# Six places for the down weights, gate products on GpSimd, and a wait ahead of each pair's inverse data, in an adaLN block of state-space convolution and gated feed-forward

## The chip, the cores and the metric

The kernel runs on one core of a Trainium2 chip. The metric is the device time of one execution in microseconds. The engines are named as the profile names them: PE is TensorE (PEld its weight load), DVE is VectorE, ACT is ScalarE, POOL is GpSimd, and SP is SyncE, whose queue issues nearly all transfers.

## The reference

The inputs are 2,048 tokens of 640 channels in float32. Cut to what matters:

```python
sa, ca, ga, sb, cb, gb = (silu(c) @ w_mod) split in six rows of 640
h = layernorm(x) * (1 + ca) + sa
x = x + ga * (causal_conv(h, K) + h * D_skip)     # K from the state-space parameters, conv by rfft/irfft of 4096
h = layernorm(x) * (1 + cb) + sb
gate, up = h @ w1, h @ w3                         # 640 -> 1728
x = x + gb * ((silu(gate) * up) @ w2)             # 1728 -> 640
```

All is float32. The kernel keeps that precision in the feed-forward part by splitting each operand in a high and a low part, so that each product is three matmuls: high by high, high by low, low by high.

## The kernel before, in words

**The convolution** takes the first 355 us. It is done channel block by channel block with transforms written as matmuls, and its instructions have an order written out by hand. The change touches nothing there. At its end the spectra's last transform step is still open: for each of 16 token slots (128 tokens each) the data lies in DRAM, in `zd`, and needs a last small product, which is added to the residual `x2`. Four consecutive slots make one block of 512 tokens. `inverse_load` (line 578 and after, transfers at line 589) fetches such data for some slots into the tile `low`, and `inverse` (line 593 and after) makes the products `iy` (line 604) and has DVE add them to `x2` (line 609). Slots 0 to 3, block 0, are done at once. Slots 4 to 15 are done as pairs of slots u = 2 to 7, inside the feed-forward of blocks 0 and 1.

**The feed-forward** treats blocks 0 and 1 in `ffn`. For each of 14 tiles of the 1,728 hidden columns (13 of 128, one of 64) it loads three weights (`wr` holds w1 and w3, `w2r` holds w2), splits them (ACT makes the high part `wh`, `w2h`; DVE the low part `wl`, `w2l`), makes gate and up in PSUM (`gu`, lines 1044 to 1046), gates them on ACT and DVE, and adds the tile's down product to five accumulators `acc` (line 1081). After each tile the function `between` is called. There, in block 0, tiles 2 to 7 and 9 to 13 each do half a pair by `inverse_half`, and block 1's first tile does the last half: an even call loads the pair's data (eight transfers) and makes the products of the first 320 channels, the odd one those of the other 320. Two pairs fit into `low` at once, as each pair uses the place `u % 2`. `between` also loads the residual `x` of blocks 2 and 3.

These loads go through `held_back`: they carry a wait for one matmul, `self.hold`, which is set once, to the last product of slots 0 to 3. `load_x2` (line 575) has it too.

**Blocks 2 and 3** are treated together. `pair_up` makes gate and up of both blocks with a scheme that saves products (lines 834 to 917), for which POOL makes sums of weights (lines 853 to 856). `pair_down` then makes the down products, first block 2's 14 tiles, then block 3's. Its weights w2 are loaded again: `load` fetches two at once into a tile `wq` of the tag `wr`, which has two such tiles, so that four weights have a place. The first four are asked for ahead of the loop; then, after each second weight is split, the next two. `weights2` splits a weight: ACT makes `w2h` (line 1029), DVE `w2l` (line 1033), each with two buffers. In block 3 the weight's first 512 columns are multiplied by the gate row `gb` before (line 1028, DVE), so that its output needs no gating.

**Block 2's output** is made by `output2`, called in the first round of block 3: ACT scales the last 128 columns, PE turns them, DVE multiplies four accumulators by the gate (line 1014) and adds the turned columns to the residual (line 1020). The four additions of line 1019 and the store (line 1018) are handed back as a list, one step to a round of block 3. Block 3's accumulators are two banks of the tag `gu` and the banks `acc0`, `acc1` and `acc4`.

**What sets the order.** Behind the convolution no order is written out. The framework puts each engine's instructions in a sequence by their priority (the program order) and by when it reckons them ready, so a load can be issued earlier than a call that stands ahead of it. Each engine, and SP's queue, then runs its sequence strictly in order.

Of the kernel before, what the change touches and what calls it, by code (L numbers as in the profile page):

```python
# [10 lines left out]
F32 = mybir.dt.float32  # L11
# [3 lines left out]
ALU = mybir.AluOpType  # L15
# [3 lines left out]
P = 128  # L19
L = 2048  # L20
D = 640
KT = D // P
# [150 lines left out]
class Plan:  # L173
# [4 lines left out]
    def add(self, name, eng, took, f, after=(), rank=0.0, port=False, take=(), give=(), table=None, dma=None):  # L178
        assert name not in self.tasks, name
        if not isinstance(eng, tuple):  # L180
            eng, f = (eng,), f and (lambda e, f=f: f())
        self.tasks[name] = (eng, f, tuple(after))
        self.takes[name] = [name + "'" * i for i, x in enumerate(take) if x[0] == "bank"]
        for tag, key in give:
            if tag == "bank":
                self.gives.setdefault(key, []).append(name)
# [24 lines left out]
class K:  # L211
# [402 lines left out]
    def inverse_half(self, i, ps, tag, bufs):  # L614

        u, h = 2 + i // 2, i % 2
        if h == 0:
            self.zu = self.inverse_load(u % 2 * 2560, 2 * u, 2, 0, D)
        self.inverse(2 * u, 2, self.zu, ps, tag, bufs, 0, D, h)


    def split(self, H, Lo, v, eng):
# [322 lines left out]
    def pair_down(self, wp, pool, ps, po):  # L945

        order = (0, 1, 2, 3, 13) + tuple(range(4, 13))
        pend = n = None
        late = []
        raw = {}  # L950
        todo = [(b, m) for b in (2, 3) for m in order]

        def load(i):
            if i % 2 == 0:
                t = self.wrp.tile([P, 2, KT, P], F32, name=f"wq{i}", tag="wr", bufs=2).rearrange("p a k f -> p a (k f)")
                for x in range(2):
                    b, m = todo[i + x]
                    raw[b, m] = t[:, x]
                    if m < 13:
                        self.nc.sync.dma_start(t[:, x], self.w2[m * P:(m + 1) * P, :])  # L960
                    else:
                        for y in range(2):
                            self.nc.sync.dma_start(t[y * 64:(y + 1) * 64, x], self.w2[1664:1728, :])
        load(0)
        load(2)
        for b in (2, 3):
            acc = None
            for m in order:
                w2h, w2l = self.weights2(b, m, wp, raw.pop((b, m)))
                i = todo.index((b, m)) + 3  # L970
                if i < len(todo):
                    load(i)
                if acc is None:
                    new = [po.tile([P, 512], F32, name=f"acc{b}{k}", tag=f"acc{k}") for k in range(KT)] if b == 2 else None
                if m < 13:
                    n = 0 if n is None else n + 1
                    t = self.slots[n % 4]
                    ah, al = t[:, :512], t[:, 512:]
                    self.split(ah, al, self.a.pop((m, b)), self.nc.vector)
                else:  # L980
                    ah, al = self.a.pop((m, b)), None
                end = (b, m) == (3, 12)
                if pend is not None:
                    self.down(*pend, *([(4, 0, 1, 2)] if end else []))
                    if acc is None and b == 3:
                        late = self.output2(pend[1], pool, ps)
                    elif late:
                        late.pop(0)()
                if acc is None:
                    acc = new or [ps.tile([P, 512], F32, name=f"acc3{k}", tag="gu", bufs=3) if k < 2 else  # L990
                                  po.tile([P, 512], F32, name=f"acc3{k}", tag=f"acc{(0, 0, 0, 1, 4)[k]}") for k in range(KT)]
                prev = pend
                pend = (m, acc, ah, al, w2h, w2l)
        real = self.nc
        nc = self.nc = Engines(self, real)
        self.down(*pend, (4, 0, 1))
        pt = self.turn_last(3, acc, ps)
        self.down(*pend, (2,))
        self.down(*prev, (3,))
        self.down(*pend, (3,))  # L1000
        self.output(3, acc, ps, pt)
        self.nc = real


    def output2(self, acc, pool, ps):

        nc = self.nc
        V = nc.vector
        x = self.x2[2]
        pt = self.turn_last(2, acc, ps)  # L1010
        y = [(pool.tile([P, 512], F32, name=f"y2{j}", tag="s", bufs=3) if j else
              self.keep.tile([P, 512], F32, name="og20", tag="og", bufs=2)) for j in range(4)]
        for j in range(4):
            V.tensor_mul(y[j], acc[j], self.gb)

        def store():
            for q in range(4):
                nc.sync.dma_start(self.ov[q, :, 8:12, :], x[q * 32:(q + 1) * 32])
        add = lambda j: V.tensor_add(x[:, j, :512], y[j], x[:, j, :512])
        V.tensor_add(x[:, :, 512:], pt, x[:, :, 512:])  # L1020
        return [lambda: add(0), lambda: add(1), lambda: add(2), lambda: add(3), store]

    def weights2(self, b, m, wp, w2r):

        nc = self.nc
        w2h, w2l = (wp.tile([P, D], F32R, name=f"w2{x}{b}_{m}", tag=f"w2{x}", bufs=2) for x in "hl")
        if b == 3:
            nc.vector.tensor_mul(w2r[:, :512], w2r[:, :512], self.gb)
        nc.scalar.activation(w2h, w2r, AF.Copy)
        q = slice(0, P if m < 13 else 64)  # L1030
        if m == 13:
            nc.gpsimd.memset(w2l[64:].bitcast(F32), 0.0)
        nc.vector.tensor_tensor(w2l[q], w2r[q], w2h[q].bitcast(F32), op=ALU.subtract)
        return w2h, w2l
# [914 lines left out]
```

## Time and profile before

| what | us |
|---|---|
| three timed runs | 944.38, 941.34, 939.71 |
| their median | 941.34 |
| the profiled execution | 938.05 |
| its span, from the first to the last instruction | 936.3 |

The profiled execution is one run of its own. Its span leaves out the 1.75 us that lie around the instructions. Times within the trace count from the span's start. By this clock the convolution ends near 355 us, `ffn` runs to near 660, `pair_up` to near 830, and `pair_down` to the end. The mean granted TensorE clock was 0.984. In rows of instructions the columns are start, duration, engine, line, operation, output from inputs, shape and count; a bracket holds the engine's idle time just before and what ended it.

### The profile page before, as it was taken

How to read it: one execution, taken by the hardware profiler on the slowest of the kernel's cores; microseconds unless marked ns; L12 is line 12 of the kernel's file. 1: busy time of each engine (PE TensorE's matmuls, PEld its weight loads, DVE VectorE, ACT ScalarE, POOL GpSimd, SP SyncE). 2: the span in 40 equal slices, each digit the busy share in tenths (PEclk: the TensorE clock that was granted, in tenths of full speed). 3: DMA queues.
4: the chain of work that ended last, by engine and by line, in shares of the span. 5: the costliest groups of instructions: out<-in, count | busy, mean ns of one | idle time of the engine just before them, and what ended most of it. 6: DMA issues, size and time to landing. Idle time of an engine off the chain costs nothing.

```text
span 936.3 us, 21994 instructions
## 1 busy us (share of the span) xinstructions
PE 846.5 (90%) x8983; PEld 673.8 (72%) x8983; DVE 693.9 (74%) x1228; ACT 518.7 (55%) x892; POOL 325.2 (35%) x323
## 2 busy tenths in 40 slices
PE   1266888999989988999999999999999999999997
PEld 1045767778778745677877788888888888888775
DVE  7899999999979756556765757465667777765753
ACT  5889999999887533423423335354333434444331
POOL 2398989998988261000000000001133333100000
PEclk9987999999999999999999999999999999999999
DMA  8966566232251469955533353231322122123342
GB/s 196 303 218 156 177 154 162 69 107 70 69 150 46 139 193 234 232 166 141 155 101 97 104 164 85 84 104 51 75 67 57 56 57 57 43 61 108 97 129 83
DMA packets 125005, 112.78 MB, mean 120 GB/s; under 512 B 12393, under 2 KB 107113, under 8 KB 123625
## 3 DMA queue, kind: packets, MB, share of 16 engines
q1 hardware_dynamic: 124136, 110.46, 42.6%
q8 instruction: 70, 1.15, 0.5%
q10 hardware_dynamic: 768, 0.92, 0.4%
q14 instruction: 31, 0.25, 0.1%
HBM read 90.38 MB, written 20.97 MB: 119 GB/s over the span
## 4 chain that ended last, share of the span: by engine, by line
PE 64%; DVE 8%; ACT 8%; DMA 7%; issue 3%; SPq 0%; POOL 0%; DVEq 0%; ACTq 0%
PE p L834 17%; PE acc L1081 16%; PE gu L1044 6%; PE gu L1046 6%; PE gu L1045 6%; PE ps L147 4%; ACT tr L147 2%; PE fz L147 2%; DMA low<-zd 2%; DVE fp L147 2%; DVE yy L147 2%; PE kps L147 2%; DMA wq<-in_w 2%; PE fk L147 1%; DMA x<-in_x 1%
## 5 line engine op out<-in xcount | busy, mean ns | idle before, releaser
L1044 PE MATMUL gu<-xh,wh 128*128 128x512 f32 x270 | 106.2, 398 | 2.8 <-ACT xh L623 1.4
L1046 PE MATMUL gu<-xh,wl 128*128 128x512 f32 x270 | 105.4, 391 | 0.0
L1045 PE MATMUL gu<-xl,wh 128*128 128x512 f32 x270 | 105.2, 390 | 0.0
L147 ACT ACTIVATE tr<-ph 128x512 f32<-128x512 f32 (+1 forms) x160 | 93.8, 603 | 8.8 <-POOL ph L147 3.9
L853 POOL TENSOR_TENSOR ws<-wp 128x256 f32<-128x256 f32 x13 | 9.6, 738 | 230.9 <-DMA wp<-in_w 116.0
L147 POOL TENSOR_TENSOR ph<-p,p 128x1024 int32<-128x1024 int32 x40 | 79.1, 1978 | 3.7 <-ACT tr L147 3.0
L147 DVE TENSOR_TENSOR yy<-yy,tr 128x512 f32<-128x512 f32 (+1 forms) x80 | 75.5, 946 | 2.6 <-ACT tr L147 2.3
L737 ACT ACTIVATE wh<-wr 128x640 fp32r<-128x640 f32 x51 | 34.9, 731 | 71.0 <-PE gu L1045 55.6
L834 PE MATMUL p<-x,wch 128*128 128x512 f32 x208 | 68.3, 389 | 0.0
L1044 PEld LDWEIGHTS gu<-xh,wh 128*128 128x128 f32 x270 | 50.6, 188 | 19.1 <-issue 2.1
L147 POOL TENSOR_TENSOR yy<-e,e 128x512 f32<-128x512 f32 x48 | 52.6, 1107 | 23.6 <-ACT e L147 16.3
L1046 PEld LDWEIGHTS gu<-xh,wl 128*128 128x128 f32 x270 | 50.7, 188 | 11.2 <-DVE wl L747 0.4
L1045 PEld LDWEIGHTS gu<-xl,wh 128*128 128x128 f32 x270 | 50.7, 188 | 10.2 <-DVE xl L624 0.2
L147 DVE TENSOR_TENSOR xx<-tr,xx 128x512 f32<-128x512 f32 x80 | 54.3, 683 | 2.0 <-ACT tr L147 1.9
L750 POOL MEMSET w2l<- 64x640 f32 x1 | 0.6, 628 | 158.4 <-PE acc L1081 158.4
L871 DVE TENSOR_TENSOR s<-p,s 128x512 f32<-128x512 f32 x52 | 34.8, 684 | 26.9 <-ACT s L869 22.9
L147 PE MATMUL kps<-yy,xx 128*32 128x64 f32 x2560 | 47.7, 224 | 5.5 <-DVE xx L147 3.7
L147 PE MATMUL ps<-wk,xb 128*64 128x128 f32 x640 | 48.3, 298 | 4.4 <-DVE hb L147 1.4
L1059 DVE TENSOR_TENSOR a<-a,gu 128x512 f32<-128x512 f32 x26 | 17.9, 687 | 45.0 <-PE gu L1046 44.8
L1057 ACT ACTIVATE th<-gu 128x512 f32<-128x512 f32 x26 | 15.5, 597 | 64.3 <-PE gu L1046 64.3
L147 PE MATMUL fh<-sp,wb 128*64 128x128 f32 x640 | 45.2, 286 | 6.3 <-issue 2.2
L147 PEld LDWEIGHTS ps<-wk,xb 128*64 128x64 f32 x640 | 43.1, 220 | 9.0 <-DVE hb L147 2.6
(381 smaller groups left out, 2352.1 us busy)
## 6 DMA issues: line engine op xcount, KB each, us to landing
wr<-in_w SPq DMA_DIRECT2D x52, 320.0 KB, 3.6
zd<-zt SPq DMA_DIRECT2D x39, 256.0 KB, 3.5
w2r<-in_w SPq DMA_DIRECT2D x26, 320.0 KB, 2.9
wp<-in_w SPq DMA_DIRECT2D x26, 320.0 KB, 3.2
wq<-in_w SPq DMA_DIRECT2D x26, 320.0 KB, 3.4
low<-zd SPq DMA_DIRECT2D x48, 160.0 KB, 5.3
xs<-in_x SPq DMA_DIRECT2D x16, 320.0 KB, 10.7
hs<-hb SPq DMA_DIRECT2D x20, 256.0 KB, 3.7
```

The source lines that it names most:

```text
L147: self.prev = self.k.order(f(*a, **kw), self.prev)
L737: self.nc.scalar.activation(wh[:, i], raw[:, i], AF.Copy)
L750: self.nc.gpsimd.memset(w2l[64:].bitcast(F32), 0.0)
L834: nc.tensor.matmul(to, t[:, o], y[:, k], start=start and k == i == 0, stop=stop and (k, i) == (n - 1, 2), skip_group_check=True)
L853: G.tensor_tensor(s[0], a21, a22, op=ALU.add)
L871: add = lambda o, bk, s: V.tensor_tensor(o, bk, s, op=ALU.add)
L1044: nc.tensor.matmul(pg, wh[:, k, :], xh[:, k, :], start=(k == 0), stop=False)
L1045: nc.tensor.matmul(pg, wh[:, k, :], xl[:, k, :], start=False, stop=False)
L1046: nc.tensor.matmul(pg, wl[:, k, :], xh[:, k, :], start=False, stop=(k == KT - 1))
L1057: nc.scalar.activation(th, gu[0], AF.Tanh, scale=0.5)
L1059: nc.vector.tensor_mul(a, a, gu[1])
L1081: nc.tensor.matmul(acc[k], *two(a, w), start=(m == 0 and i == 0), stop=(m == 12 and i == 2))
```

## The change

The change has two parts.

1. `inverse_half` keeps the last matmul of a pair's first half as the new `self.hold`. The loads of the next pair, and block 3's residual, thereby wait for that matmul, where they waited for the last product of slots 0 to 3.
2. `pair_down` has six places for weights: the four halves of the two `wr` tiles, and two tiles of the tag `w2r`. Each weight is loaded alone, six ahead of its use, into the place of the weight just split. The gate product of `weights2` goes from DVE to POOL. In `output2`, two of the four gate products are made at once and two in the next rounds, the addition of the turned columns comes a round later still, and the four additions go from DVE to POOL.

```diff
@@ inverse_half
-        self.inverse(2 * u, 2, self.zu, ps, tag, bufs, 0, D, h)
+        i = self.inverse(2 * u, 2, self.zu, ps, tag, bufs, 0, D, h)
+        if h == 0:
+            self.hold = i
@@ pair_down
-        raw = {}
         todo = [(b, m) for b in (2, 3) for m in order]
+        room = []
+        for i in range(2):
+            t = self.wrp.tile([P, 2, KT, P], F32, name=f"wq{i}", tag="wr", bufs=2).rearrange("p a k f -> p a (k f)")
+            room += [t[:, 0], t[:, 1]]
+        room += [self.wrp.tile([P, D], F32, name=f"wq{i}", tag="w2r", bufs=2) for i in (2, 3)]
 
         def load(i):
-            if i % 2 == 0:
-                t = self.wrp.tile([P, 2, KT, P], F32, name=f"wq{i}", tag="wr", bufs=2).rearrange("p a k f -> p a (k f)")
-                for x in range(2):
-                    b, m = todo[i + x]
-                    raw[b, m] = t[:, x]
...
-        load(0)
-        load(2)
+            m, t = todo[i][1], room[i % 6]
+            if m < 13:
+                self.nc.sync.dma_start(t, self.w2[m * P:(m + 1) * P, :])
+            else:
+                for y in range(2):
+                    self.nc.sync.dma_start(t[y * 64:(y + 1) * 64], self.w2[1664:1728, :])
+        for i in range(6):
+            load(i)
...
-                w2h, w2l = self.weights2(b, m, wp, raw.pop((b, m)))
-                i = todo.index((b, m)) + 3
-                if i < len(todo):
-                    load(i)
+                i = todo.index((b, m))
+                w2h, w2l = self.weights2(b, m, wp, room[i % 6])
+                if i + 6 < len(todo):
+                    load(i + 6)
@@ output2
-        for j in range(4):
+        def gated(j):
             V.tensor_mul(y[j], acc[j], self.gb)
+
+        def add(j):
+            nc.gpsimd.tensor_tensor(x[:, j, :512], y[j], x[:, j, :512], op=ALU.add)
...
-        add = lambda j: V.tensor_add(x[:, j, :512], y[j], x[:, j, :512])
-        V.tensor_add(x[:, :, 512:], pt, x[:, :, 512:])
-        return [lambda: add(0), lambda: add(1), lambda: add(2), lambda: add(3), store]
+        gated(0)
+        gated(1)
+        return [lambda: (gated(2), add(0)), lambda: (gated(3), add(1)),
+                lambda: (V.tensor_add(x[:, :, 512:], pt, x[:, :, 512:]), add(2)), lambda: add(3), store]
@@ weights2
-            nc.vector.tensor_mul(w2r[:, :512], w2r[:, :512], self.gb)
+            nc.gpsimd.tensor_tensor(w2r[:, :512], w2r[:, :512], self.gb, op=ALU.mult)
```

More of the change, by code (lines that the diff above doesn't have):

```diff
@@ L949, in pair_down @@
         late = []
-        raw = {}
         todo = [(b, m) for b in (2, 3) for m in order]
-        def load(i):
-            if i % 2 == 0:
-                t = self.wrp.tile([P, 2, KT, P], F32, name=f"wq{i}", tag="wr", bufs=2).rearrange("p a k f -> p a (k f)")
-                for x in range(2):
-                    b, m = todo[i + x]
-                    raw[b, m] = t[:, x]
[L959 to L963, printed above, removed]
-        load(0)
-        load(2)
+        room = []
[3 more added lines that the diff above has]
+        room += [self.wrp.tile([P, D], F32, name=f"wq{i}", tag="w2r", bufs=2) for i in (2, 3)]
+        def load(i):
+            m, t = todo[i][1], room[i % 6]
[6 more added lines that the diff above has]
+            load(i)
         for b in (2, 3):
```

## The prediction

> **What bounds the kernel now.** I read the page's busy times first, then the tensor engine's waits from 376 us on, then the same stretch in windows, because all that the change touches runs after about 375 us: the loads of inverse data in the feed-forward loop of block 0, and the down products of blocks 2 and 3.
>
> ```profile
> PE 846.5 (90%) x8983; PEld 673.8 (72%) x8983; DVE 693.9 (74%) x1228; ACT 518.7 (55%) x892; POOL 325.2 (35%) x323
> ```
> ```profile
> PE acc L1081 <- DVE w2l L1033: 2.4, 3, 1.0
> PE gu L1044 <- DVE x L609: 1.1, 1, 1.1
> ```
> ```profile
> 880.00:928.00 48.00, 45.61 (x200) 36.49 (x199) 29.28 (x44) 14.25 (x22) 0.63 (x1) 1.00 0.30 96
> sum 552.00, PE 548.29 PEld 442.79 DVE 358.19 ACT 216.31 POOL 48.03; mean PE 137.07 PEld 110.70 DVE 89.55 ACT 54.08 POOL 12.01
> ```
>
> The waits read "who waited, for whom: us in total, times, longest"; the windows read length, then busy time of PE, PEld, DVE, ACT and POOL, the granted clock, the DMA share and GB/s; the last row sums all windows from 376 to 928 us. There PE is busy in 548.29 of 552 us. Four waits count: one of 1.1 us on an addition of inverse data, and three, 2.4 us together, on the low part of a down weight. This caps what the change can win: the 3.7 us that PE is not busy, plus what the modelled end of the matmul before each wait hides. I give each its own cause, since the change has a part for either.
>
> **The wait at 395 us.** SP's queue, then the engines round it (start, duration, engine, line, operation, count, and in brackets idle time and what ended it):
>
> ```profile
> 375.05 2.24 SPq L575 DMA_DIRECT2D x<-in_x  x4
> 377.60 8.38 SPq L589 DMA_DIRECT2D low<-zd  x8
> 386.15 9.14 SPq L720 DMA_DIRECT2D wr<-in_w  x6
> ...
> 405.56 3.00 SPq L589 DMA_DIRECT2D low<-zd  x5
> ```
> ```profile
> 389.89 0.74 PE L604 MATMUL iy<-low,x_low 64*32 64x320 f32 x6
> ...
> 391.94 1.52 ACT L737 ACTIVATE wh<-wr 128x640 fp32r<-128x640 f32 x2 [8.98 <-DMA wr<-in_w]
> 392.72 1.60 DVE L747 TENSOR_TENSOR wl<-wr,wh 128x640 fp32r<-128x640 f32 x2 [8.31 <-ACT wh L737]
> ...
> 395.38 0.50 PE L1044 MATMUL gu<-xh,wh 128*128 128x512 f32 x1 [1.14 <-DVE x L609]
> ```
>
> The eight `low` loads at 377.60 are pair u=3's. The first `wr` load waits behind them on SP until 386.15. ACT then idles 8.98 us for those weights, DVE 8.31 us for ACT, and DVE's addition of pair u=2's products stands behind that on DVE's own queue. PE needs the PSUM bank which that addition frees. u=3's data was in no hurry:
>
> ```profile
> 413.62 0.70 PE iy L604 x16
> ```
>
> This step of the chain that ended last is the first half of u=3's products. What was loaded at 377.60 was first used 36 us later.
>
> **What the hold does.** Each load of a pair u=3..7, 40 `low` DMAs, and the four `x` loads of block 3 (line 575 asks `held_back` too), now waits for the last matmul of the older pair's first half. For u=3 this is 389.89 + 0.74 = 390.63 by the row. The 2.24 and 8.38 us of issues at 375.05 and 377.60 leave SP's path, so the `wr` loads can go about 8 us sooner, as soon as DVE has freed their buffer. PE then finds the bank free: the gain is the 1.14 us of wait; by starts of matmuls it is more. Two undisturbed ones, and the last before the wait:
>
> ```profile
> 377.06 0.39 PE L1044 MATMUL gu<-xh,wh 128*128 128x512 f32 x1
> 377.29 0.39 PE L1045 MATMUL gu<-xl,wh 128*128 128x512 f32 x1
> ...
> 393.85 0.39 PE L1046 MATMUL gu<-xh,wl 128*128 128x512 f32 x1
> ```
>
> Undisturbed matmuls start 0.23 us apart (377.06, 377.29), here 395.38 - 393.85 = 1.53, so 1.30 is lost. What the hold adds: SP waits in order, and behind a held `low` load stand `wr` and `w2r` loads. Issued at 391, u=3's loads have 22 us to their use at 413.62; the five issued at 405.56 took 3.00 us of issue, so eight take 4.8. Later pairs are likewise asked for two halves of products ahead of their use. Block 3's `x` loads wait for the same matmul, and are first needed by pair u=6. I book that at nothing; the cover is those 22 us, and without it each us late is a us of PE. An extra semaphore wait per load isn't shown apart; between nothing and 0.1 us of SP each it is hidden too.
>
> **The three waits at 884, 898 and 910 us.** PE's rows; one of DVE's; and DVE's gate products as a group (busy, mean ns, idle before them):
>
> ```profile
> 883.56 0.39 PE L1081 MATMUL acc<-w2h,wch 128*128 128x512 f32 x1
> 884.95 0.50 PE L1081 MATMUL acc<-wch,w2l 128*128 128x512 f32 x1 [1.00 <-DVE w2l L1033]
> ...
> 896.64 1.07 PE L1081 MATMUL acc<-w2h,wcl 128*128 128x512 f32 x4
> 898.53 0.50 PE L1081 MATMUL acc<-wcl,w2l 128*128 128x512 f32 x1 [0.82 <-DVE w2l L1033]
> ...
> 908.20 1.07 PE L1081 MATMUL acc<-w2h,wch 128*128 128x512 f32 x4
> 909.83 0.50 PE L1081 MATMUL acc<-wch,w2l 128*128 128x512 f32 x1 [0.57 <-DVE w2l L1033]
> ```
> ```profile
> 880.49 1.88 DVE L1014 TENSOR_TENSOR y<-acc,gb 128x512 f32<-128x512 f32 x3
> ```
> ```profile
> L1028 DVE TENSOR_TENSOR wq<-wq,gb 128x512 f32<-128x512 f32 x14 | 9.7, 690 | 13.5 <-DMA wq<-in_w 13.5
> ```
>
> By starts (four matmuls in a group start 0.23 apart, so the last begins 0.68 after the first) the losses are 1.16, 1.89 - 0.68 - 0.23 = 0.98, and 1.63 - 0.91 = 0.72: 2.86 us, where the waits say 2.39. DVE multiplies each weight of block 3 by the gate, and blocks there until the weight has landed, 13.5 us in all; the low part `w2l` of an earlier weight stands behind. At 884 no transfer is late: the gating and adding of block 2's output fill DVE.
>
> **What part two does to them.** How long the weights took to land:
>
> ```profile
> DMA to landing us min/median/max: 2.7/3.3/4.6
> ```
>
> Six places instead of four, each refilled as soon as its low part is made, let a load go six weights ahead. A weight is 15 matmuls, 15 x 0.23 = 3.4 us, so about 20 us, against 2.7 to 4.6 us to land. The gate's 14 products and four sums go to POOL, where such operations took:
>
> ```profile
> L147 POOL TENSOR_TENSOR yy<-e,e 128x512 f32<-128x512 f32 x48 | 52.6, 1107 | 23.6 <-ACT e L147 16.3 <-PE kps L147 3.9 <-issue 2.5
> ...
> L624 POOL TENSOR_TENSOR xl<-v,xh 128x512 fp32r<-128x512 f32 x2 | 3.0, 1518 | 16.9 <-ACT xh L623 16.9
> ```
>
> DVE sheds 18 x 0.690 = 12.4 us and 13.5 us of blocking. POOL takes 18 x 1.107 = 19.9 us up to 18 x 1.518 = 27.3; no row shows the very operation, and I take the lower, which has its shape and output type. POOL is busy 0.63 us in the window from 880, so it has room. The gating stays between landing and split, but some 20 us ahead of its use. Without that cover it would add up to 1.5 us to every weight. On POOL's own queue the products stand behind one memset of `w2l`, which waits for PE, and behind the four sums; that delays one weight, inside the lead. The store of block 2 leaves SP later than now; five weights after 884 it is 901, far ahead of the last products at 928. Of `output2`, two products of four and the last columns move behind the next weights, and no bank that block 3 takes waits for them.
>
> What POOL costs DVE is seen in the stage before:
>
> ```profile
> L914 DVE TENSOR_TENSOR a<-a,c x4: 1221/1224/1226, 679.3 to 717.7; 128x512 f32<-128x512 f32 x4
> ...
> L914 DVE TENSOR_TENSOR a_x<-a_x,c x2: 685/688/691, 815.4 to 827.1; 128x512 f32<-128x512 f32 x2
> ```
>
> The same product takes 1.224 us where POOL's sums of weights run beside it and 0.688 us where they do not: 0.54 more. In block 3 two DVE operations per weight read two SBUF tiles, the low parts of activation and weight. The Trainium skill, GPSIMD Engine Reference, Key points, says that GpSimd shares its SBUF interfaces with VectorE and collides with instructions that have two SBUF inputs; this trace agrees with these two rows, and by that rule the move is little relief to DVE. From the rows, 18 x 0.54 = 9.7 of DVE's 12.4 us would come back if each of POOL's operations met one of DVE's. Block 2, which has no gating, shows the slack:
>
> ```profile
> 859.31 0.82 DVE L1033 TENSOR_TENSOR w2l<-wq,w2h 128x640 fp32r<-128x640 f32 x1
> ```
> ```profile
> 862.58 0.39 PE L1081 MATMUL acc<-wch,w2l 128*128 128x512 f32 x1
> ```
>
> The low part is done at 860.13 and PE wants it at 862.58: 2.45 us of slack. Both operations beside POOL cost 2 x 0.54 = 1.08, so the waits stay away.
>
> **Sum.** 1.30 + 2.86 = 4.16, say 4.2 us; the waits alone say 3.5. The profiled execution took 938.05 us (span 936.3, 1.75 outside it), so it would become 933.9. It ran 3.29 us under the median of the three timed runs, 941.34; from that the forecast is 937.1 us. What is late next is PE itself, without a gap until the last products.
>
> **Rivals.** *More than the profile shows* (0.14): the timed runs are 1.7 to 6.3 us longer than the profiled one. If those 3.29 us of the median are the same waits for transfers, made longer, they go too: 941.34 - 4.2 - 3.3 = 933.8. For it: all but one of the waits hang on transfers. Against: the first 355 us, untouched, are full of transfers too.
>
> *Part one does nothing* (0.12): the `wr` load waits for its buffer or for its share of the transfers anyway, or the order of some other queue makes the same loss. Then 941.34 - 2.9 = 938.4. For it: the twelve issues took 10.6 us, near 0.9 each, against 0.6 for the five at 405.56, so the queue was backed up, and the weights share it. Against: the load left SP within 0.2 us of the end of the last `low` issue (377.60 + 8.38 = 385.98).
>
> *POOL and DVE slow each other* (0.08): if the products fall into the chain from landing to PE, a weight costs 1.5 + 1.08 more than in block 2, 2.6 us against 2.45 of slack, and the waits stay in smaller or equal number. The gain is 1.3 at most: 940.0. It needs the lead of six weights to be lost, say by POOL's queue standing at the memset.
>
> *The new wait sits ahead of the weights on SP* (0.11), which ends slower. Program order has the weight load of that round before u=3's loads, but the trace of before shows them issued the other way round, so the order isn't given by the code. If the twelve issues kept their place and now waited until 390.63, the first `wr` would go after 2.24 + 4.8 us more, at 397.7 instead of 386.15, 11.5 us late (15 with the 8.38 us of the row at 377.60). DVE's addition, and with it PE's restart at 395.38, moves as far: 941.34 - 2.9 + 11.5 = 949.9. It decides from the point where the first `wr` leaves later than 386.15 - 1.3 = 384.9.
>
> **Chances.** A difference of about 0.5%, 4.7 us here, is what a measurement of this kernel can tell from none. The forecast has 0.55; it lies just short of that bound, and with the floor of gaps between 3.5 and 4.5 and a run's scatter 0.22 of it falls beyond. Faster: 0.22 + 0.14 = 0.36. Same: 0.33 + 0.12 + 0.08 = 0.53. Slower: 0.11. The range leaves out the slower rival and goes from the larger gain, 933.8, rounded down to 933.5, up to 940.0 plus 2.0, nearly half of the spread of the runs before (944.38 - 939.71): 942.0. The forecast's own range is 935.5 to 939.
>
> **What would show it.** Right: the first `wr` of that stretch leaves SP before 385, u=3's `low` loads after u=2's first products, no wait of PE for `x L609` near 395; no wait of DVE for `wq`, 14 products on POOL ahead of their weights, no wait of PE for `w2l`, and PE busy in all of 880 to 925. Wrong: a held load on SP with idle ACT behind it; POOL waiting at the memset with DVE waiting for POOL; or new waits of PE between 376 and 820, where PE has one of a microsecond now, through another order on some queue.

## The result, and the profile after

The changed kernel took 935.76 us, the median of seven runs (935.31 to 939.99), and the kernel before 943.88 us (seven runs, 939.71 to 947.44; three of them are the runs known at the prediction, with the median 941.34). These two medians lie 8.1 us apart. The ratio on record, which I go by, says less: it is 0.9941, 95% interval 0.9916 to 0.9965, or 5.6 us shorter, with 3.3 and 7.9 as ends. That is 0.59%, so the bound of 0.5% lies inside the interval. A second measurement of the same two kernels gave 0.9945 (0.9925 to 0.9966). The forecast was 937.1. In the experiments below, one execution each of two kernels (e2, 1,408 us; e9, 1,964 us) lies far outside the others and counts in no ratio.

Read the page's first line as before, then PE's waits from 376 us to the end (who waited, for whom: us in total, times, longest), then the last of the windows and their sum, which now run from 376 to 925.6 us. All three are of the profiled execution after, which took 935.73 us, with a span of 933.9.

```profile
PE 847.4 (91%) x8983; PEld 674.6 (72%) x8983; DVE 691.8 (74%) x1210; ACT 519.2 (56%) x892; POOL 352.9 (38%) x341
```
```profile
PE gu L1050 <- DVE a L1064: 0.2, 1, 0.2
```
```profile
877.00:925.60 48.60, 48.59 (x218) 39.69 (x218) 29.63 (x32) 16.59 (x26) 20.12 (x14) 1.00 0.29 87
sum 549.60, PE 549.30 PEld 444.61 DVE 356.24 ACT 218.12 POOL 75.06; mean PE 137.32 PEld 111.15 DVE 89.06 ACT 54.53 POOL 18.77
```

Of the waits on `x L609` and on `w2l` none is left: PE stands for 0.3 us in 549.6, where it stood for 3.7 in 552. This is the floor of PE that the prediction named as what is late next.

The queue of SP around the old wait at 395 us, with DVE's, ACT's and PE's rows beside it:

```profile
380.53 9.14 SPq L722 DMA_DIRECT2D wr<-in_w  x6
...
393.22 1.73 SPq L575 DMA_DIRECT2D x<-in_x  x4
394.99 6.84 SPq L589 DMA_DIRECT2D low<-zd  x8
```
```profile
385.67 1.37 ACT L739 ACTIVATE wh<-wr 128x640 fp32r<-128x640 f32 x2 [0.21 <-PE gu L1051]
386.82 1.55 DVE L749 TENSOR_TENSOR wl<-wr,wh 128x640 fp32r<-128x640 f32 x2
...
390.34 0.48 DVE L609 TENSOR_TENSOR x<-iy,x 128x320 f32<-128x320 f32 x1
...
392.38 0.74 PE L604 MATMUL iy<-low,x_low 64*32 64x320 f32 x6
...
414.60 0.77 PE L604 MATMUL iy<-low,x_low 64*32 64x320 f32 x16
```

The order has turned round. The `wr` loads leave at 380.53, ahead of the pair's data; ACT no longer idles for them (its bracket says 0.21 us, for PE); and `wl` is done before DVE's addition is due. The held loads leave when u=2's products of the first half end, at 392.38 + 0.74 = 393.12: first block 3's `x`, then u=3's eight `low` loads, whose data is used at 414.60.

**Why one pair of spans doesn't show the gain.** 936.3 to 933.9 is only 2.4 us. These rows are the first feed-forward matmul, before and after:

```profile
365.31 0.98 PE L1044 MATMUL gu<-xh,wh 128*128 128x512 f32 x3 [1.40 <-ACT xh L623]
```
```profile
367.82 0.98 PE L1050 MATMUL gu<-xh,wh 128*128 128x512 f32 x3 [1.40 <-ACT xh L625]
```

The part that the change doesn't touch ended 2.51 us later in the profiled execution after. From that first matmul to the span's end it took 936.3 - 365.31 = 571.0 us before and 933.9 - 367.82 = 566.1 after: 4.9 us less. I call this length **the stretch**; it is what I compare between profiles from here on. It is still one execution each, while the ratio is made of many.

### The profile page after: what moved, and what is told of

Same layout as the page of the kernel before. It is cut to its first block, busy times and chain, and to the rows that moved or that the text cites. A ratio compares the mean times of both kernels' runs of the same rounds, so it can differ in the third digit from the quotient of the medians.

```text
span 933.9 us, 22012 instructions
## 1 busy us (share of the span) xinstructions
PE 847.4 (91%) x8983; PEld 674.6 (72%) x8983; DVE 691.8 (74%) x1210; ACT 519.2 (56%) x892; POOL 352.9 (38%) x341
## 4 chain that ended last, share of the span: by engine, by line
PE 72%; ACT 10%; DVE 9%; issue 4%; DMA 2%; POOL 1%; SPq 1%; ACTq 0%; DVEq 0%
PE acc L1087 20%; PE p L836 17%; PE gu L1050 7%; PE gu L1052 7%; PE gu L1051 7%; PE ps L147 4%; ACT tr L147 3%; DVE yy L147 3%; PE fz L147 2%; PE kps L147 2%; PE fk L147 2%; ACT hn L147 2%; DVE xx L147 2%; DVE fp L147 2%; PE fh L147 1%
```

## The experiments

The theory is the prediction's: four gaps of PE go, each through the part made for it. Two rivals offer reasons why more than the 4.2 us of the sum might go: that these waits are longer in most executions than in the one profiled, or that the runs differ by something ahead of the feed-forward. Later experiments take each part to pieces. All of them in one table; the ratio is to the kernel before on the same chip, PE's waits are those from 376 us on for additions (`x L609`) and down weights (`w2`).

| kernel | ratio (95%) | stretch, us | PE's waits, us |
|---|---|---|---|
| before | | 571.0 | x 1.1; w2 2.4 |
| e3_before_again | 1.0007 (0.9988 to 1.0026) | 572.6 | x 2.2; w2 2.9 |
| after | 0.9941 (0.9916 to 0.9965) | 566.1 | none |
| e4_after_again | 0.9945 (0.9925 to 0.9966) | 566.2 | w2 0.2 |
| e1_hold_alone | 1.0006 (0.9980 to 1.0032) | 570.8 | w2 3.8 |
| e2_down_alone | 0.9968 (0.9941 to 0.9996) | 568.8 | x 2.3 |
| e5_six_dve | 1.0007 (0.9987 to 1.0028) | 569.0 | w2 2.1 |
| e6_four_pool | 0.9970 (0.9954 to 0.9986) | 568.1 | w2 0.4 |
| e12_hold_four_pool | 0.9982 (0.9949 to 1.0016) | 567.4 | w2 0.8 |
| e10_dve_in_turn | 0.9965 (0.9933 to 0.9997) | 565.8 | none |
| e11_add_first | 0.9960 (0.9939 to 0.9981) | 565.8 | none |
| e7_hold_second | 0.9998 (0.9982 to 1.0014) | 574.6 | see there |
| e8_weights_held | 0.9939 (0.9915 to 0.9963) | 569.3 | iy 0.5 |
| e9_pool_twice | 1.0028 (1.0008 to 1.0047) | | |

### Both kernels again, and each part alone

No edit in the first two. In the third, `inverse_half` alone is changed; the fourth is the changed kernel without that.

```diff
@@ e1_hold_alone against before
-        self.inverse(2 * u, 2, self.zu, ps, tag, bufs, 0, D, h)
+        i = self.inverse(2 * u, 2, self.zu, ps, tag, bufs, 0, D, h)
+        if h == 0:
+            self.hold = i
@@ e2_down_alone against after
-        i = self.inverse(2 * u, 2, self.zu, ps, tag, bufs, 0, D, h)
-        if h == 0:
-            self.hold = i
+        self.inverse(2 * u, 2, self.zu, ps, tag, bufs, 0, D, h)
```

> The kernel before, unchanged, for a second profile and as a control of the comparison. All theories: ratio 1.000 within 0.2%. Theory 1: the four waits again sum to 3.5 us, within 0.5, in this profile. Theory 2: in an execution that is longer than 938 us the four waits are longer by the same amount. Theory 3: the waits are the same and the first feed-forward matmul starts at another time than 365.3 us, by as much as the whole execution differs.

> The changed kernel, unchanged, for a second comparison. Theory 1: 4.2 us faster, ratio 0.9955 (0.994 to 0.997). Theory 2: 5.5 us or more, ratio 0.992 to 0.994. Theory 3: time from the first feed-forward matmul to the end is 566.1 us again, within 0.5, and the ratio scatters about 0.9950 with the start of that matmul.

> Part one alone (the hold), the down part as before. Theory 1, four gaps: the change is worth the four waits of PE that the profile before shows, and each part its own: the wait near 395 us is gone, the three on the low down weight near 884, 898 and 910 stay, so 1.3 us faster, ratio 0.9986 (0.998 to 0.9995). Theory 2, waits that are longer in most runs than in the one profiled: 2 to 4 us faster, ratio 0.996 to 0.998, as this wait hangs on backed-up transfers. Theory 3, the surplus is scatter of the convolution: as theory 1 in the feed-forward, whatever the whole time says.

> Part two alone (six places, products and sums on POOL), no new hold. Theory 1: the wait near 395 stays with some 1.1 us, the three in the down products are gone, 2.9 us faster, ratio 0.997 (0.9955 to 0.998). Theory 2: 3 to 5 us faster, ratio 0.995 to 0.997. Theory 3: as theory 1 from the first feed-forward matmul on.

PE's waits in e3, then in e1, then in e2:

```profile
PE acc L1081 <- DVE w2l L1033: 2.9, 5, 0.9
PE gu L1044 <- DVE x L609: 2.2, 1, 2.2
```
```profile
PE acc L1083 <- DVE w2l L1035: 3.8, 5, 1.1
```
```profile
PE gu L1048 <- DVE x L609: 2.3, 1, 2.3
```

In these profiles each part takes away its own waits and leaves the other's: e1 has no wait for `x L609`, e2 none for `w2l`. The waits themselves vary. The down weights cost 2.4 us in three waits in the profiled execution of before, 2.9 and 3.8 in five here. By starts of matmuls, worked out as in the prediction, e3 loses 2.33 near 395 and 3.73 in the down products, 6.1 us, where the profile before showed 4.2.

The wait near 395 us varies most, and it isn't always there. Five profiles have neither the new hold nor another order on DVE: before, e2, e3, and two from further down, e5 and e6. SP's first `wr` row after the pair's data, in e5 and then in e2:

```profile
388.90 8.55 SPq L720 DMA_DIRECT2D wr<-in_w  x6
```
```profile
392.05 9.57 SPq L720 DMA_DIRECT2D wr<-in_w  x6
```

Counted from each run's first feed-forward matmul, that load leaves SP after 18.8 us in e6, 19.2 in e5, 20.8 in before, 21.6 in e2 and 22.4 in e3, and PE waits 0, 0, 1.1, 2.3 and 2.2 us. The prediction put the bound at 384.9 us, which is 19.6 us after the first matmul; the five agree with it. In after, e4, e1, e7, e10 and e12, which all have a hold, the load leaves after 12.7 us each time, and none of them has the wait. So part one takes away a delay that costs PE between nothing and 2.3 us, as an execution falls. That the waits are longer in most executions than in the one profiled isn't shown: two of the five are longer near 395, two have none.

The third explanation holds for spans: the first feed-forward matmul started anywhere from 365.31 to 370.46 us. By time, part two alone gives 0.9968. Part one's worth doesn't show in time: e1 against before (1.0006), after against e2 and e12 against e6 differ both ways, inside their intervals.

### Part two: places or engine?

e5 keeps the six places and puts the products and the additions back on DVE, without part one. e6 is the reverse: the four places of before, with the products and the additions on POOL. e12 is e6 with part one.

```diff
@@ e5_six_dve against e2 (with output2 as before)
-            nc.gpsimd.tensor_tensor(w2r[:, :512], w2r[:, :512], self.gb, op=ALU.mult)
+            nc.vector.tensor_mul(w2r[:, :512], w2r[:, :512], self.gb)
@@ e6_four_pool against before (with output2 as after)
-            nc.vector.tensor_mul(w2r[:, :512], w2r[:, :512], self.gb)
+            nc.gpsimd.tensor_tensor(w2r[:, :512], w2r[:, :512], self.gb, op=ALU.mult)
@@ e12_hold_four_pool against e6
+        i = self.inverse(2 * u, 2, self.zu, ps, tag, bufs, 0, D, h)
+        if h == 0:
+            self.hold = i
```

> Six places, but the gate products and the sums stay on DVE, and no new hold. From the first feed-forward matmul to the end of the span the kernel before took 571.0 and 572.6 us in two profiles, the changed one 566.1 and 566.2. Theory A, transfers: DVE's wait for weights is what delays the low parts, and the places cure it. Then DVE waits for wq under 2 us in all, PE's waits for w2l near 871, 898, 905 and 910 are gone, and only the one near 884, which is DVE's own load, stays with about 1 us; the wait near 395 stays; that stretch takes about 569.5 us. Theory B, engine: the move to POOL is what counts. Then at least two of the waits besides the one near 884 stay, and the stretch takes 571 us or more.

> Gate products and sums on POOL, but four places filled by twos, and no new hold. Theory A, transfers: the products of weights that come late are now POOL's wait instead of DVE's, and the split behind them comes later by POOL's longer product (1.5 instead of 0.69 us): waits of PE for w2l of 2 us or more in all stay, the stretch from the first feed-forward matmul takes 570 us or more. Theory B, engine: DVE is free and no wait for w2l over 0.3 us is left; 568.8 us, as with both in part two alone.

> The hold, and gate products and sums on POOL, but four places filled by twos. Theory sequence and engine: the six places bring nothing of their own; as the changed kernel, ratio 0.994 to 0.996, at most 0.5 us of PE waiting for a split near 900. Rival, lead: with POOL's longer product the lead of two to three weights isn't enough; 1 us or more of waits, ratio 0.996 or more.

e5: PE's waits; DVE's gate products as a group (busy, mean ns, idle before them); then one row of ACT's timeline and two of DVE's:

```profile
PE acc L1081 <- DVE w2l L1033: 2.1, 4, 0.7
```
```profile
L1028 DVE TENSOR_TENSOR wq<-wq,gb 128x512 f32<-128x512 f32 x14 | 9.7, 690 | 11.5 <-DMA wq<-in_w 11.3
```
```profile
906.76 0.72 ACT L1029 ACTIVATE w2h<-wq 128x640 fp32r<-128x640 f32 x1
```
```profile
910.84 0.69 DVE L1028 TENSOR_TENSOR wq<-wq,gb 128x512 f32<-128x512 f32 x1 [2.38 <-DMA wq<-in_w]
911.45 0.82 DVE L1033 TENSOR_TENSOR w2l<-wq,w2h 128x640 fp32r<-128x640 f32 x1
```

Six places without POOL bring no gain that shows: 1.0007, four waits for `w2l` against three and five in before and e3, and DVE waits 11.3 us for weights where it waited 13.5. (The stretch of 569.0 is shorter than before's because this execution had no wait near 395 us, where one was expected.) The last two rows show one of the four. The low part at 911.45 subtracts the high part that ACT had ready at 906.76 + 0.72 = 907.48; it stands behind the product of a later weight, for which DVE waited 2.38 us, and PE then waits 0.7 us for it. The likely reason, which e10 tests: a product stands in DVE's sequence at about the time at which the framework reckons its load to be there. Asking for the load earlier moves the product up as well, so it goes on standing ahead of nearer work.

POOL without the places gives what both gave: 0.9970 against 0.9968. PE's waits in e12, then ACT's for POOL in e6:

```profile
PE acc L1087 <- DVE w2l L1039: 0.4, 1, 0.4
PE acc L1087 <- ACT w2h L1035: 0.4, 1, 0.4
```
```profile
ACT w2h L1033 <- POOL wq L1032: 6.6, 2, 4.2
```

What the places add on top is at most these last waits: 0.4 us in e6 and 0.8 in e12, against none and 0.2 in the two profiles of the changed kernel. e12's interval holds both no change and after's ratio, so the times can't settle a difference of that size.

### The products on DVE, in turn

e10 has the hold, six places, and all of part two's work on DVE again, but each product stands in DVE's sequence behind the low part of the weight two before it. This sets an order on one engine and adds no wait.

```diff
@@ e10_dve_in_turn against after (with output2 as before)
-            nc.gpsimd.tensor_tensor(w2r[:, :512], w2r[:, :512], self.gb, op=ALU.mult)
+            x = nc.vector.tensor_mul(w2r[:, :512], w2r[:, :512], self.gb)
+            self.order(x, self.lows[-2])
...
-        nc.vector.tensor_tensor(w2l[q], w2r[q], w2h[q].bitcast(F32), op=ALU.subtract)
+        self.lows.append(nc.vector.tensor_tensor(w2l[q], w2r[q], w2h[q].bitcast(F32), op=ALU.subtract))
```

> With the hold and six places, gate products and sums back on DVE, but each product is put in DVE's sequence behind the low part of the weight two before, without a wait. Theory sequence: what stalled DVE was not the engine but the place of the product, put ahead of nearer low parts as soon as its load is reckoned landed; behind them it finds its weight landed, so DVE waits for wq under 1 us in all and PE's waits for w2l are gone but the one near 884 (up to 1.2 us). The stretch takes 566.5 to 567.5 us. Rival, engine: DVE has no room for 14 more products, PE waits 2 us or more in all; 568.5 us or more.

DVE's products as a group, and PE's waits:

```profile
L1031 DVE TENSOR_TENSOR wq<-wq,gb 128x512 f32<-128x512 f32 x14 | 9.5, 682 | 0.0
```
```profile
PE gu L1048 <- DVE a L1062: 0.2, 1, 0.2
```

DVE waits for no transfer of a weight, PE for no `w2l`, and the stretch is 565.8, against 566.1 of after. DVE has the time for all this work. What hurt was the product's place in the queue, and POOL cured that by being another queue.

### Part one: late weights, or what stands behind them?

e11 has no hold. It puts the low parts of the fifth tile's weights (`m` = 3) behind DVE's addition of u=2's first products, again by order alone. e8 goes the other way: it is the changed kernel with those weights' loads held as well, until that pair's first products are done, which goes most of the way to what the slower rival foretold.

```diff
@@ e11_add_first against e2
-                    nc.vector.tensor_add(x2, py[p][:, :n], x2)
+                    y = nc.vector.tensor_add(x2, py[p][:, :n], x2)
+                    if part == 0:
+                        self.added = y
...
-                eng.tensor_tensor(wl[:, i], raw[:, i], wh[:, i].bitcast(F32), op=ALU.subtract)
+                x = eng.tensor_tensor(wl[:, i], raw[:, i], wh[:, i].bitcast(F32), op=ALU.subtract)
+                if (b, m) == (0, 3):
+                    self.order(x, self.added)
@@ e8_weights_held against after, weights_load
-        dma = ... if b == 0 and m == 1 else nc.sync.dma_start
+        dma = ... if b == 0 and m == 1 else (lambda *a: self.held_back(nc.sync.dma_start(*a))) if b == 0 and m == 3 else nc.sync.dma_start
```

> Part two alone (no new hold), but DVE's low parts of the fifth tile's weights are put in its sequence behind the addition of pair u=2's first products, without a wait; the loads leave SP in the order of before. Theory sequence: PE's wait near 395 comes from DVE standing at late weights ahead of an addition that is ready; with the addition first it is gone, though the weights are as late as before. No wait of PE for x L609 over 0.3 us, 566.2 us from the first feed-forward matmul (without the clock's dips). Rival, transfers: PE then waits a little later for the late weights themselves, 1 us or more; 567 to 569 us.

> The changed kernel, and the first weight load behind pair u=2's data (w1, w3 and w2 of the fifth tile of block 0) carries the same wait for u=2's first products. This is the slower rival's place in a small form. That rival's price: the load leaves at about 391 instead of 380.5 us (counted from a start of 367.8 us of the first feed-forward matmul), and each us beyond 384.9 on the clock of before, 387.4 here, is a us of PE: some 4 us lost, the stretch takes 570 us, with a wait of PE for x L609 or for the weights. Rival: PE's sequence has enough other work there (down products of the tile before); less than 1 us lost, 566 to 567 us.

e11: SP's queue, DVE's, and PE's matmul for which the addition must be done:

```profile
381.11 8.12 SPq L589 DMA_DIRECT2D low<-zd  x8
389.39 3.77 SPq L722 DMA_DIRECT2D wr<-in_w  x4
```
```profile
396.46 0.69 DVE L626 TENSOR_TENSOR al<-a,ah 128x512 fp32r<-128x512 f32 x1 [8.65 <-ACT ah L625]
397.07 0.48 DVE L609 TENSOR_TENSOR x<-iy,x 128x320 f32<-128x320 f32 x1
...
398.99 1.55 DVE L749 TENSOR_TENSOR wl<-wr,wh 128x640 fp32r<-128x640 f32 x2
```
```profile
397.61 0.50 PE L1052 MATMUL gu<-xh,wh 128*128 128x512 f32 x1
```

SP has the order of before, and the weights leave as late as before: 389.39 is 20.6 us after this run's first feed-forward matmul (368.76), 386.15 was 20.8 after. Yet PE doesn't wait, because the 1.55 us of `wl` no longer stand ahead of the addition. It is only just enough: the addition ends at 397.55 and PE's matmul starts at 397.61. And the late weights still hold DVE, by another way: `al`, next ahead of the addition, waits 8.65 us for ACT, which makes its input behind the late weights' `wh`. So this one profile shows the part that `wl`'s place plays; it doesn't show that weights as late as in e2 or e3 would do no harm in this order. e8: SP's rows, DVE's, and PE's wait:

```profile
396.90 0.96 SPq L717 DMA_DIRECT2D wr<-in_w  x2
```
```profile
396.90 0.49 DVE L609 TENSOR_TENSOR x<-iy,x 128x320 f32<-128x320 f32 x1 [1.27 <-PE iy L604]
...
400.73 0.82 DVE L749 TENSOR_TENSOR wl<-wr,wh 128x640 fp32r<-128x640 f32 x1 [2.21 <-ACT wh L739]
```
```profile
PE iy L604 <- DVE a L1064: 0.5, 1, 0.5
```

Here the weights leave at 396.90, 27.2 us after the first matmul (369.72), 6.3 us later than in before. PE waits 0.5 us, once, at 419.55, for another operation of DVE, and the ratio is after's own, 0.9939. DVE has its additions ahead of `wl` here. I take it that the framework knew of the wait, since it is in the program, when it laid the sequence; that is argued, not shown. (The stretch of 569.3 holds some 3 us at half clock at its start, from 369.72 on; more of that below.)

### The hold half a pair later

e7 holds on the second half's last product, so that the next pair is asked for one call later.

```diff
-        if h == 0:
+        if h == 1:
             self.hold = i
```

> The changed kernel, but the hold is the older pair's second half: each pair's data is asked for one half of a pair, 11 us, ahead of its use instead of 22. The prediction's account of the cover: eight issues (4.9 us) and 4.4 us of landing are 9.3 us, so later pairs just come in time, and pair u=3, behind four loads of x and in a backed-up queue, comes 1 to 3 us late for PE; the stretch takes 567 to 570 us. Rival: the loads are in time all the same, as the products can be moved behind other matmuls in PE's sequence; 566.2 us, no wait of PE for low or x over 0.3 us.

PE's timeline, and windows (length; busy time of PE, PEld, DVE, ACT, POOL; granted clock; DMA share; GB/s):

```profile
414.58 4.82 PE L604 MATMUL iy<-low,x_low 64*32 64x320 f32 x14
419.33 0.79 PE L1050 MATMUL gu<-xh,wh 128*128 128x512 f32 x1
419.93 0.63 PE L1051 MATMUL gu<-xl,wh 128*128 128x512 f32 x1
420.35 0.63 PE L1052 MATMUL gu<-xh,wl 128*128 128x512 f32 x1
```
```profile
415.00:420.00 5.00, 4.85 (x16) 1.36 (x15) 1.35 (x3) 0.48 (x1) 0.00 (x0) 0.80 1.06 277
420.00:425.00 5.00, 5.00 (x12) 2.75 (x11) 1.43 (x5) 0.00 (x0) 0.00 (x0) 0.50 0.25 88
425.00:430.00 5.00, 5.00 (x17) 3.93 (x16) 0.69 (x1) 0.60 (x1) 0.00 (x0) 0.68 0.00 0
```

The data left SP from 406.11 on, 8.5 us ahead of its use where after has 19.6. The products then take 4.82 us where after's row at 414.60 has 0.77: 4.05 us lost. And it isn't over there: the clock is 0.50 in the next window, matmuls start 0.42 us apart (419.93, 420.35) instead of 0.23. The stretch is 8.5 us longer than after's, and the ratio is 0.9998: one late pair took back the whole gain. The merged rows show as busy what is waiting; only the durations tell.

### Twice the work on POOL

e9 makes each gate product on POOL twice, the first time into a scratch tile that nobody reads.

```diff
         if b == 3:
+            nc.gpsimd.tensor_tensor(self.scr, w2r[:, :512], self.gb, op=ALU.mult)
             nc.gpsimd.tensor_tensor(w2r[:, :512], w2r[:, :512], self.gb, op=ALU.mult)
```

> The changed kernel with each gate product on POOL made twice, once more into a scratch tile. POOL's product took 1.5 us there, so POOL has 3 us of each weight's 3.4, and meets DVE's two operations of a weight nearly always: these took 1.77 and 1.92 us where they met POOL, 3.7 us a weight if both do, against 3.4 us of PE. Theory contention decides: DVE becomes late and PE waits for w2l again, 2 to 5 us in all; the stretch from the first feed-forward matmul takes 568 to 571 us instead of 566.2. Rival, cover holds: the meetings stay partial, DVE has 2.45 us of slack a weight, no wait over 0.5 us; 566 to 567 us.

e9 left no profile that can be set beside the others, so only its times are used here. They give the ratio 1.0028: some 8 us slower than after by the two ratios (1.0028 - 0.9941 = 0.0087 of 942). So POOL's work does reach the end once there is twice as much of it; through which wait, this run doesn't show.

## Why the prediction was right, and which steps were off

**Right: the mechanism.** Both parts did what the prediction said, and the four gaps went. The first `wr` left SP at 380.53, before 385; u=3's loads after u=2's first products; DVE never waits for `wq`; PE is busy throughout the last window.

**Not settled: the sum of 4.2 us.** The terms 1.30 and 2.86 were read rightly from one execution, but one execution can't size them. The same two places cost 2.33 and 3.73 in e3, and the first cost nothing in e5 and e6. The measured gain of 5.6 us (3.3 to 7.9) lies between the forecast's 4.2 and the 7.5 of the rival *more than the profile shows* (941.34 - 933.8), and its interval holds both. The second measurement's 5.2 us (3.2 to 7.1) holds 4.2 and just leaves out 7.5. That the time of 935.8 came so near the 937.1 is in part luck: the wait near 395 us in the profile taken lay between the extremes. The chances put "within 0.5%" ahead of "faster", 0.53 to 0.36; at 0.59% with 0.5% inside the interval, the measurement doesn't decide between them.

**Wrong in the reason: "six places ... let a load go six weights ahead".** The lead is real, if shorter than "some 20 us". These are POOL's first product in after, and the first of the fourteen splits of block 3's weights by ACT, which is of that same weight:

```profile
861.00 1.39 POOL L1034 TENSOR_TENSOR wq<-wq,gb 128x512 f32<-128x512 f32 x1 [17.05 <-DMA wq<-in_w]
```
```profile
876.66 0.72 ACT L1035 ACTIVATE w2h<-wq 128x640 fp32r<-128x640 f32 x1
```

From the product's start to that split it is 15.7 us. But e5 has the places and keeps the waits, e6 lacks them and is rid of nearly all, e10 shows the cause. In e5's rows the weight of the late low part was there; the product of a later weight stood ahead of it in DVE's queue. The prediction had the sentence, "DVE ... blocks there until the weight has landed ...; the low part of an earlier weight stands behind", and then credited the lead with the cure.

**Right, with more than one link: the wait at 395.** The prediction's chain ran from the `low` loads ahead of `wr` to late weights, to ACT and DVE standing for them, to the addition behind `wl`. The five profiles without the hold show the first links: PE waits where the weights leave past the bound, and not where they leave ahead of it. e11 leaves the weights late and takes only `wl` out of the addition's way; that was enough by a hair. With weights that are later still, but with the additions ahead of `wl`, e8 does no harm worth counting.

**Wrong end: POOL's price.** I took 1.107 us, and the upper bound of 1.518 was right. POOL's groups after (busy, mean ns, idle before), and beside them POOL's and DVE's timeline at the one place where both are full:

```profile
L1034 POOL TENSOR_TENSOR wq<-wq,gb 128x512 f32<-128x512 f32 x14 | 21.2, 1517 | 35.6 <-DMA wq<-in_w 35.6
L1019 POOL TENSOR_TENSOR x<-y,x 128x512 f32<-128x512 f32 x3 | 4.7, 1592 | 0.0
```
```profile
885.80 1.74 POOL L1019 TENSOR_TENSOR x<-y,x 128x512 f32<-128x512 f32 x1
887.70 1.68 POOL L1034 TENSOR_TENSOR wq<-wq,gb 128x512 f32<-128x512 f32 x1 [0.16 <-DMA wq<-in_w]
891.91 1.29 POOL L1034 TENSOR_TENSOR wq<-wq,gb 128x512 f32<-128x512 f32 x1 [2.54 <-DMA wq<-in_w]
```
```profile
886.31 1.92 DVE L1039 TENSOR_TENSOR w2l<-wq,w2h 128x640 fp32r<-128x640 f32 x1
888.15 1.78 DVE L626 TENSOR_TENSOR wch<-awl,wch 128x512 fp32r<-128x512 f32 x1
889.85 0.81 DVE L1039 TENSOR_TENSOR w2l<-wq,w2h 128x640 fp32r<-128x640 f32 x1
```

**Mis-sized: contention of 0.54 us.** Undisturbed, `w2l` takes 0.81 us (889.85); at 886.31 it takes 1.92, 1.1 more, twice what I took from the sums of weights at L914. Two such operations, 1.92 and 1.78 against 0.82 and 0.69, cost a weight 2.2 us. Against the slack of 2.45 that left little; the rival *POOL and DVE slow each other* was nearer than its 0.08. That e9 is some 8 us slower fits it, though its place isn't shown.

**Not as the diff reads: `output2`.** Two of its gate products were to come a round later. All four ran one behind the other on DVE from 878.38 us on: the framework pulled them forward. No number of the sum hung on it.

**Wrong price: the slower rival.** It let each us of a late `wr` become a us of PE. In e8 `wr` is 7.6 us past that rival's threshold (27.2 us after the first matmul, where 384.9 is 19.6; some 1.8 us of it come of the slow clock at the start, as u=2's first products end 27.1 us after the first matmul there and 25.3 in after), and 0.5 us of wait came of it at most. The price missed that DVE's sequence can change with the wait. That the harm in before came of a sequence that expected the weights sooner than they came fits e8 and e11, and is argued.

**Right, and tested: the cover of 22 us** for the held loads. It was 19.6; with 8.5 in e7 a stall of 4.05 us comes, and the stretch grows by 8.5: twice the foretold price of "each us late is a us of PE".

## What to carry to other kernels

When an engine runs its queue in order and its bracket names a DMA, look at what stands behind that instruction: if it is ready work for the bottleneck engine, more buffers may change nothing, while another engine's queue or a later place in the same queue cures it. Take the size of a small gain from several executions, since the wait near 395 us was absent in two runs and 2.3 us in another, and compare from a point where the runs are in step. And give a delayed load its cover in us ahead of its use: 20 did no harm here, 8.5 cost the whole gain.

## What the runs showed of the hardware

**DVE and POOL take turns.** In the rows above, POOL's addition ends at 885.80 + 1.74 = 887.54; DVE's `w2l`, begun at 886.31, ends 0.69 after that, at 888.23. POOL's next product ends at 889.38, and DVE's next one 0.55 later, at 889.93. Each time DVE's operation takes about its own time, counted from the end of POOL's. The Trainium skill, SBUF — State Buffer, SBUF: two separate sides, says that the port pair shared by DVE and GpSimd is locked for a whole instruction and the other side blocks in full. These rows agree: the extra 1.1 us is close to what POOL's instruction still had to run at 886.31 (1.23 us). So do the others: in all 18 rows of after, e4, e6 and e12 in which a product or sum of POOL ends while a `w2l` is under way, the `w2l` ends 0.67 to 0.69 us later.

**A stall of PE costs more than itself.** After the 4.05 us of e7 the granted clock was 0.50 for the window from 420 and 0.68 in the next. The Trainium skill, TensorE: Matmul & The Clock Gate, Part 1, has the clock halved after an idle window of about 3.4 us; this run agrees, though PE still made fourteen small products meanwhile. The waits of 1.1 to 2.3 us near 395 us in before, e3 and e2 left the clock at 1.00.

**The same code starts at another clock.** The twenty transposes just ahead of the feed-forward, in after and in e4, which are the same kernel, and the window around them:

```profile
364.01 2.40 PE L657 MATMUL tp<-ident,xn 128*128 128x128 f32 x20 [2.54 <-ACT xn L641]
```
```profile
364.34 4.07 PE L657 MATMUL tp<-ident,xn 128*128 128x128 f32 x20 [2.54 <-ACT xn L641]
```
```profile
365.00:370.00 5.00, 3.91 (x19) 3.60 (x18) 2.15 (x3) 2.73 (x6) 0.00 (x0) 0.69 1.01 229
```

After has a clock of 1.00 in that window, e4 0.69. In e6 and e8 the dip reaches into the first feed-forward matmuls, whose first three take 1.65 us there and 0.98 in after. The transposes alone make 1.7 us between two executions of one kernel, as much as the wait that part one is made for.
